# Linear attention into a GELU MLP on one core: a rebuilt opening with idle matmuls on zeros, own PSUM banks for the transposes, and two edits to the schedule of chunk preparation

## Chip, cores, metric

One core of a Trainium2 chip. The metric is the device time of one launch in microseconds (us), median of several runs. A profiled execution gives the trace. Its span, from the first to the last instruction, is some 2 us shorter than the time measured for the same execution.

## The reference

```python
# q, k, v: (4, 8, 768, 64); lam: (8,); w_in: (512, 2048); w_out: (2048, 512)
for b in range(nb):                       # blocks of 64 rows
    intra = (qb @ kb.T * Dmask) @ vb      # Dmask: lam**(i-j) on and below the diagonal
    inter = (qb * lam_pow) @ kv_state
    out[:, :, sl] = intra + inter
    kv_state = lam_block * kv_state + (kb * rev_pow).T @ vb
x = out, transposed to (3072, 512)
y = gelu_exact(x @ w_in) @ w_out          # (3072, 512), float32
```

## The kernel before

The kernel works in chunks of 128 rows: 24 chunks, six to a batch entry, so chunks 0, 6, 12 and 18 start from an empty state and chunks 5, 11, 17 and 23 need no new one. Four chunks make a group of 512 rows, which then goes through the MLP. The attention of the next group's chunks is woven between the MLP's matmuls of the present group.

Each chunk has these steps: loads of k, q, v on GpSimd's DMA queue; kT and qT (by TensorE for chunks 0 to 7, by a DMA transpose of k and of q_hat = q x decay for the later ones); k_dec = k x decay; scores; the product kv = k_decT v and the new state; outputs. GpSimd issues the loads and computes k_dec, q_hat and `old` (the decayed state). It executes all of this in program order.

The opening (chunks 0 to 3), cut:

```python
    def transposes(c):
        t_ps = bank([128, 2, HP, C], BF16, "mh" if c.early else "t", "t_ps")   # k and q in one bank
        ...
    def scores(c):        # scores, then kv, then masks, then the state: all in one function
        ...
    for s in range(M + 2):
        if s < M:
            live[s] = begin(s, early=True)
            if s == 2:
                load_w_in(0)
            transposes(live[s])
            decay_k(live[s], nc.scalar if s < 2 else nc.gpsimd)
            ...
        if 0 <= s - 1 < M:
            scores(live[s - 1])
        if s >= 2:
            outputs(live[s - 2], xT[0], s - 2)
```

The schedule of the later chunks, cut. A position is a fraction of a group's matmul work:

```python
    for n in range(M, NCH):
        g, i = n // M - 1, n % M
        first, end = (0.66, 1.0) if g == 0 else (0.0, 0.97)
        at = lambda f: (g + first + (end - first) * (i + f) / M) * total
        fs = (-0.5, 0.0, 0.5, 1.05) if g == 0 else (-1.0, 0.0, 0.35, 0.75)
        todo += [(at(f), kind, n) for kind, f in enumerate(fs)]
    todo.sort()

    def step(kind, n):
        g = n // M - 1
        if kind == 0:                      # preparation of chunk n
            live[n] = begin(n)
            if g > 0:
                dma_transposes(live[n])    # q_hat on GpSimd, two DMA transposes
            decay_k(live[n], nc.gpsimd)
            prefetch(n + 5)                # loads, up to that chunk
        ...
```

Of the kernel before, what the change touches and what calls it, by code (L numbers as in the profile page):

```python
# [8 lines left out]
F32 = mybir.dt.float32  # L9
BF16 = mybir.dt.bfloat16  # L10
ALU = mybir.AluOpType
ACT = mybir.ActivationFunctionType
# [3 lines left out]
def kernel(  # L16
# [10 lines left out]
    nc = tc.nc  # L27

    B, H, S, D = q.shape
    d_model, d_ff = moe_w_in.shape  # L30
    C = 128
    NB = S // C
    NCH = B * NB
    HP = H // 2
# [5 lines left out]
    M = 4  # L40
# [5 lines left out]
    consts = ctx.enter_context(tc.tile_pool(name="consts", bufs=1))  # L46
    w_pool = ctx.enter_context(tc.tile_pool(name="w", bufs=1))
    qkv_pool = ctx.enter_context(tc.tile_pool(name="qkv", bufs=8))
    work_pool = ctx.enter_context(tc.tile_pool(name="work", bufs=3))
# [13 lines left out]
    def load(n, name):  # L63
        raw[n, name] = qkv_pool.tile([128, H, D], BF16, tag=name, name=f"{name}_t")
        nc.gpsimd.dma_start(raw[n, name], chunk_of(name, n))  # L65
# [5 lines left out]
    pos = consts.tile([128, 1], F32)  # L71
# [13 lines left out]
    def load_w_in(s):  # L85
        f = d_ff // NS
        nc.gpsimd.dma_start(w_in_t[:, :, s * f:(s + 1) * f], w_in_r[:, :, s * f:(s + 1) * f])  # L87

    def load_w_out(s):
        f = NK2 // NS  # L90
        nc.gpsimd.dma_start(w_out_t[:, s * f:(s + 1) * f, :], w_out_r[:, s * f:(s + 1) * f, :])  # L91

    ident = consts.tile([128, 128], BF16)
    cmask = consts.tile([128, C], F32)
    negj = consts.tile([128, 1], F32)
    cmj = consts.tile([128, 1], F32)
    warm = consts.tile([128, 1], F32)
# [8 lines left out]
    lam_q = consts.tile([128, HP, C], F32)  # L106
# [3 lines left out]
    lam_c = consts.tile([128, HP], F32)  # L110
# [12 lines left out]
    lam_c_b = lam_c[:, :, None].to_broadcast((128, HP, D))  # L123

    def make_dmask():
        nc.vector.tensor_mul(dmask, cmask[:, None, :].to_broadcast((128, H, C)),
                             lam_m[:, :, None].to_broadcast((128, H, C)))
# [5 lines left out]
    xT = {}  # L133
    states = {}

    def bank(shape, dtype, tag, name):
        return ps.tile(shape, dtype, tag=tag, name=name, bufs=2 if tag in ("sc", "mh", "mo") else 1)

    def begin(n, early=False):
        c = Chunk()  # L140
        c.n, c.sb, c.early = n, n % NB, early
        c.sc_tag = "mo" if early and n % 2 else "sc"
        c.q, c.k, c.v = (raw.pop((n, name)) for name in "qkv")
        return c

    def decay_k(c, eng):

        if c.sb == NB - 1:
            return
        c.k_dec = work_pool.tile([128, H, D], BF16, tag="kd", name="k_dec")  # L150
        if eng is nc.scalar:
            for h in range(H):
                nc.scalar.activation(c.k_dec[:, h, :], c.k[:, h, :], ACT.Copy, scale=lam_k[:, h:h + 1])
        else:
            eng.tensor_mul(c.k_dec, c.k, lam_k[:, :, None].to_broadcast((128, H, D)))  # L155

    def transposes(c):
        t_ps = bank([128, 2, HP, C], BF16, "mh" if c.early else "t", "t_ps")
        for i, src in ((0, c.k), (1, c.q)):
            for hp in range(HP):  # L160
                nc.tensor.transpose(t_ps[:, i, hp, :], src[:, 2 * hp:2 * hp + 2, :], ident)  # L161
        c.kT = work_pool.tile([128, HP, C], BF16, tag="kT", name="kT")
        c.qT = work_pool.tile([128, HP, C], BF16, tag="qT", name="qT")
        if c.early:
            nc.scalar.copy(c.kT, t_ps[:, 0])
        else:
            nc.vector.tensor_copy(c.kT, t_ps[:, 0])  # L167
        nc.vector.tensor_mul(c.qT, t_ps[:, 1], lam_q)  # L168

    def dma_transposes(c):  # L170
        c.kT = work_pool.tile([128, HP, C], BF16, tag="kT", name="kT")
        c.qT = work_pool.tile([128, HP, C], BF16, tag="qT", name="qT")
        q_hat = work_pool.tile([128, H, D], BF16, tag="qh", name="q_hat")
        nc.sync.dma_start_transpose(out=c.kT, in_=c.k.rearrange("p h d -> p (h d)"))
        nc.gpsimd.tensor_mul(q_hat, c.q, lam_p[:, :, None].to_broadcast((128, H, D)))  # L175
        nc.sync.dma_start_transpose(out=c.qT, in_=q_hat.rearrange("p h d -> p (h d)"))

    def scores(c):
        sc_ps = [bank([128, HP, C], F32, c.sc_tag, f"sc_ps{hi}") for hi in range(2)]
        for hp in range(HP):  # L180
            for hi in range(2):
                p = slice(hi * D, (hi + 1) * D)
                nc.tensor.matmul(sc_ps[hi][:, hp, :], c.kT[p, hp, :], c.qT[p, hp, :], start=True, stop=True)  # L183
        more = c.sb < NB - 1
        if more:
            kv_ps = bank([128, HP, D], F32, "t", "kv_ps")
            for hp in range(HP):
                for hi in range(2):
                    h = 2 * hp + hi
                    nc.tensor.matmul(kv_ps[hi * D:(hi + 1) * D, hp, :], c.k_dec[:, h, :], c.v[:, h, :],  # L190
                                     start=True, stop=True)
        c.sc_m = work_pool.tile([128, HP, 2, C], BF16, tag="sc_m", name="sc_m")
        dmask_r = dmask.rearrange("p (hp hi) i -> p hp hi i", hi=2)
        for hi in range(2):
            nc.vector.tensor_mul(c.sc_m[:, :, hi, :], sc_ps[hi], dmask_r[:, :, hi, :])  # L195
        if more:
            new = work_pool.tile([128, HP, D], BF16, tag="state", name="state")
            if c.sb == 0:
                nc.vector.tensor_copy(new, kv_ps)
            else:  # L200
                nc.vector.tensor_add(new, kv_ps, states[c.n][1])  # L201
            old = work_pool.tile([128, HP, D], F32, tag="old", name="old")
            if c.sb < NB - 2:
                (nc.vector if c.early else nc.gpsimd).tensor_mul(old, new, lam_c_b)  # L204
            states[c.n + 1] = new, old

    def outputs(c, x_t, off):
        o_ps = bank([128, HP, C], F32, "o", "o_ps")
        if c.sb > 0:
            for hp in range(HP):  # L210
                for hi in range(2):
                    p = slice(hi * D, (hi + 1) * D)
                    nc.tensor.matmul(o_ps[p, hp, :], states[c.n][0][p, hp, :], c.qT[p, hp, :],  # L213
                                     start=(hp == 0), stop=False, skip_group_check=True)
        for hp in range(HP):
            for hi in range(2):
                nc.tensor.matmul(o_ps[hi * D:(hi + 1) * D, hp, :], c.v[:, 2 * hp + hi, :], c.sc_m[:, hp, hi, :],  # L217
                                 start=(c.sb == 0 and hp == 0), stop=True, skip_group_check=True)
        x_o = x_t[:, :, off * C:(off + 1) * C]
        if c.early:  # L220
            nc.scalar.copy(x_o, o_ps)  # L221
        else:
            nc.vector.tensor_copy(x_o, o_ps)  # L223
# [65 lines left out]
    def prefetch(upto):  # L289
        while next_load[0] <= min(upto, NCH - 1):  # L290
            for name in "kqv":
                load(next_load[0], name)
            next_load[0] += 1
# [2 lines left out]
    alloc_x(0)  # L296
    live = {}
    make_dmask()
    for s in range(M + 2):
        if s < M:  # L300
            live[s] = begin(s, early=True)
            if s == 2:
                load_w_in(0)
            transposes(live[s])
            decay_k(live[s], nc.scalar if s < 2 else nc.gpsimd)
            if s == 1:
                nc.scalar.activation(warm, pos, ACT.Gelu)
        if 0 <= s - 1 < M:
            scores(live[s - 1])
        if s >= 2:  # L310
            outputs(live[s - 2], xT[0], s - 2)
    for s in range(1, NS):
        load_w_in(s)
    for s in range(NS):
# [5 lines left out]
    for n in range(M, NCH):  # L320
        g, i = n // M - 1, n % M
        first, end = (0.66, 1.0) if g == 0 else (0.0, 0.97)
        at = lambda f: (g + first + (end - first) * (i + f) / M) * total
        fs = (-0.5, 0.0, 0.5, 1.05) if g == 0 else (-1.0, 0.0, 0.35, 0.75)
        todo += [(at(f), kind, n) for kind, f in enumerate(fs)]
    todo.sort()

    def step(kind, n):
        g = n // M - 1
        if kind == 0:  # L330
            live[n] = begin(n)
            if g > 0:
                dma_transposes(live[n])
            decay_k(live[n], nc.gpsimd)
            prefetch(n + 5)
        elif kind == 1:
            if g == 0:
                transposes(live[n])
        elif kind == 2:
            scores(live[n])  # L340
        else:
            outputs(live[n], xT[g + 1], n % M)

# [43 lines left out]
```

## Time and profile before

| | before |
|---|---|
| time, median of 3 runs | 239.39 us (237.59 to 240.59) |
| span of the profiled execution | 237.5 us |
| TensorE busy | 209.7 us |
| first large matmul (of the MLP) | 23.6 us |
| kv of chunk 4 | 46.8 us |
| kv of chunk 6, after a wait of 9.1 us for k_dec | 64.6 us |
| first large matmul of the second group | 73.6 us |
| scores of chunk 8 | 76.3 us |

Two of these from the timeline, kv of chunk 4 and the first large matmul of the second group:

```profile
46.84 0.32 PE L190 MATMUL kv_ps<-v_t,k_dec 128*64 128x64 bf16 x8
...
73.61 2.75 PE L235 MATMUL h_ps<-x_t,w_in_t 128*128 128x512 bf16 x12 [0.79 <-DVE x_t L223]
```

The strip in the prediction shows, in 40 slices of 5.94 us, the busy share in tenths and the clock granted to TensorE. The timeline has one row for each run of like instructions: start, duration, engine, line, operation, output<-inputs, shapes, count, and in brackets the idle time before it with what ended it. Line numbers shift between kernels; the tile names do not. "Cold" means that TensorE ran at half clock, "warm" at the full one.

### The profile page before, as it was taken

The numbers are of one execution on the slowest core, as the hardware profiler recorded it, in microseconds if no ns is written. First come the engines' busy times: TensorE is split into PE (matmuls) and PEld (weight loads), VectorE is DVE, ScalarE is ACT, GpSimd is POOL, SyncE is SP. The second block draws the span as 40 slices with busy tenths as digits, with TensorE's granted clock in tenths as the row PEclk, the third lists the DMA queues.
The fourth block names the chain that finished last, engine by engine and source line by source line (L and its number), as shares of the span: only waits on it lengthen the run. The fifth ranks groups of instructions, "written<-read, shape, count | busy, mean of one in ns | idle before, by whom it ended". The sixth has DMA issues, their size and how long they took to land.

```text
span 237.5 us, 3783 instructions
## 1 busy us (share of the span) xinstructions
PE 209.7 (88%) x1528; PEld 102.5 (43%) x1552; DVE 62.7 (26%) x111; ACT 86.0 (36%) x158; POOL 111.6 (47%) x132
## 2 busy tenths in 40 slices
PE   1576999993198999999999999999999999999994
PEld 0355344441044444444444444444444444444453
DVE  3396000264034333132223213222321323100000
ACT  6862365000004552106650125621056510266211
POOL 8997236899717949901684696004403200000000
PEclk9999999999569999999999999999999999999998
DMA  7999999999985999994969999601433101110012
GB/s 51 146 149 199 202 207 159 153 188 138 149 35 135 114 88 95 134 171 110 92 56 101 109 168 170 63 0 47 134 89 68 22 26 65 44 44 0 32 59 88
DMA packets 100272, 24.36 MB, mean 103 GB/s; under 512 B 92960, under 2 KB 97312, under 8 KB 100256
## 3 DMA queue, kind: packets, MB, share of 16 engines
q0 software_dynamic: 79104, 13.64, 79.7%
q1 hardware_dynamic: 21152, 10.50, 20.2%
q8 instruction: 12, 0.20, 0.4%
q14 instruction: 4, 0.03, 0.1%
HBM read 27.27 MB, written 6.29 MB: 141 GB/s over the span
## 4 chain that ended last, share of the span: by engine, by line
PE 70%; POOL 14%; DMA 11%; issue 3%; DVE 0%; ACT 0%; POOLq 0%
PE o_ps L247 30%; PE h_ps L235 30%; DMA w_out_t<-in_moe_w_out_dram 8%; DMA k_t<-in_k_dram 3%; POOL v_t L65 3%; POOL q_t L65 3%; POOL k_t L65 3%; PE o_ps L217 3%; PE sc_ps L183 2%; PE o_ps L213 2%; POOL k_dec L155 2%; PE kv_ps L190 2%; PE o_ps L262 1%; POOL w_in_t L87 1%; POOL w_out_t L91 1%
## 5 line engine op out<-in xcount | busy, mean ns | idle before, releaser
L235 PE MATMUL h_ps<-x_t,w_in_t 128*128 128x512 bf16 x372 | 88.0, 386 | 2.3 <-DVE x_t L223 0.8
L247 PE MATMUL o_ps<-w_out_t,g_t 128*128 128x512 bf16 x356 | 83.7, 385 | 1.8 <-issue 1.7
L237 ACT ACTIVATE g_t<-h_ps 128x512 bf16<-128x512 f32 x96 | 57.3, 597 | 41.0 <-PE h_ps L235 41.0
L235 PEld LDWEIGHTS <-w_in_t 128*128 128x128 bf16 x384 | 36.8, 99 | 45.5 <-issue 4.6
L247 PEld LDWEIGHTS <-g_t 128*128 128x128 bf16 x368 | 34.4, 99 | 40.4 <-issue 1.7
L252 ACT COPY o_sb<-o_ps 128x512 f32<-128x512 f32 x23 | 13.5, 585 | 96.0 <-PE o_ps L247 87.8
L195 DVE TENSOR_TENSOR sc_m<-sc_ps,dmask 128x512 bf16<-128x512 f32 x48 | 30.9, 685 | 62.5 <-PE sc_ps L183 62.5
L204 POOL TENSOR_TENSOR old<-state,lam_c 128x256 f32<-128x256 bf16 x12 | 7.3, 611 | 61.4 <-DVE state L201 35.3
L65 POOL DMA_DIRECT2D q_t<-in_q_dram x24 | 21.4, 894 | 5.4 <-DMA w_out_t<-in_moe_w_out_dram 3.3
L65 POOL DMA_DIRECT2D k_t<-in_k_dram x24 | 22.0, 915 | 3.7 <-DMA w_out_t<-in_moe_w_out_dram 1.7
L65 POOL DMA_DIRECT2D v_t<-in_v_dram x24 | 21.3, 889 | 5.0 <-DMA w_in_t<-in_moe_w_in_dram 1.7
L223 DVE CAST x_t<-o_ps 128x512 bf16<-128x512 f32 x20 | 13.8, 690 | 35.6 <-PE o_ps L217 35.6
L155 POOL TENSOR_TENSOR k_dec<-k_t,lam_k 128x512 bf16<-128x512 bf16 x18 | 19.0, 1058 | 0.0
L175 POOL TENSOR_TENSOR q_hat<-q_t,lam_p 128x512 bf16<-128x512 bf16 x16 | 16.7, 1046 | 0.0
L190 PE MATMUL kv_ps<-v_t,k_dec 128*64 128x64 bf16 x160 | 6.9, 212 | 10.5 <-POOL k_dec L155 9.1
L217 PE MATMUL o_ps<-sc_m,v_t 128*64 128x128 bf16 x192 | 10.8, 240 | 0.0
L183 PE MATMUL sc_ps<-qT,kT 64*128 64x128 bf16 x192 | 10.4, 233 | 0.3 <-DVE qT L168 0.2
L190 PEld LDWEIGHTS <-k_dec 128*64 128x64 bf16 x160 | 4.8, 119 | 12.9 <-POOL k_dec L155 9.3
L161 PE MATMUL t_ps<-ident,k_t 128*128 128x128 bf16 x32 | 4.2, 275 | 6.8 <-DMA k_t<-in_k_dram 6.3
L183 PEld LDWEIGHTS <-kT 64*128 64x128 bf16 x192 | 6.0, 99 | 9.5 <-issue 8.0
L213 PE MATMUL o_ps<-qT,state 64*64 64x128 bf16 x160 | 8.9, 235 | 0.7 <-ACT x_t L221 0.7
L167 DVE COPY kT<-t_ps 128x512 bf16<-128x512 bf16 x4 | 1.7, 424 | 28.2 <-PE t_ps L161 28.1
(39 smaller groups left out, 70.6 us busy)
## 6 DMA issues: line engine op xcount, KB each, us to landing
out_dram<-o_sb SPq DMA_DIRECT2D x23, 256.0 KB, 2.2
k_t<-in_k_dram POOLq DMA_DIRECT2D x24, 128.0 KB, 4.4
q_t<-in_q_dram POOLq DMA_DIRECT2D x24, 128.0 KB, 5.5
v_t<-in_v_dram POOLq DMA_DIRECT2D x24, 128.0 KB, 6.1
w_in_t<-in_moe_w_in_dram POOLq DMA_DIRECT2D x4, 512.0 KB, 8.4
w_out_t<-in_moe_w_out_dram POOLq DMA_DIRECT2D x4, 512.0 KB, 15.4
kT<-k_t SPq DMA_TRANSPOSE x16, 4.0
qT<-q_hat SPq DMA_TRANSPOSE x16, 4.1
```

Of the source, the lines that this page charges most:

```text
L65: nc.gpsimd.dma_start(raw[n, name], chunk_of(name, n))
L155: eng.tensor_mul(c.k_dec, c.k, lam_k[:, :, None].to_broadcast((128, H, D)))
L175: nc.gpsimd.tensor_mul(q_hat, c.q, lam_p[:, :, None].to_broadcast((128, H, D)))
L183: nc.tensor.matmul(sc_ps[hi][:, hp, :], c.kT[p, hp, :], c.qT[p, hp, :], start=True, stop=True)
L190: nc.tensor.matmul(kv_ps[hi * D:(hi + 1) * D, hp, :], c.k_dec[:, h, :], c.v[:, h, :], start=True, stop=True)
L195: nc.vector.tensor_mul(c.sc_m[:, :, hi, :], sc_ps[hi], dmask_r[:, :, hi, :])
L213: nc.tensor.matmul(o_ps[p, hp, :], states[c.n][0][p, hp, :], c.qT[p, hp, :], start=(hp == 0), stop=False, skip_group_check=True)
L217: nc.tensor.matmul(o_ps[hi * D:(hi + 1) * D, hp, :], c.v[:, 2 * hp + hi, :], c.sc_m[:, hp, hi, :], start=(c.sb == 0 and hp == 0), stop=Tru ...
L223: nc.vector.tensor_copy(x_o, o_ps)
L235: nc.tensor.matmul(h_ps, w_in_t[:, ki, kf * 128:(kf + 1) * 128], x_t[:, ki, :], start=(ki == 0), stop=(ki == NK1 - 1))
L237: nc.scalar.activation(g_t[:, kf, :], h_ps, ACT.Gelu)
L247: nc.tensor.matmul(om[io], g_t[:, kf, io * C:(io + 1) * C], w_out_t[:, kf, :], start=(kf == 0), stop=(kf == NK2 - 1))
```

## The change

The intent by its title: TensorE should not wait idle, and at a halved clock, while the first chunks arrive. The diff has two edits more, in the schedule. Its core:

```diff
+    idle = consts.tile([128, 512], BF16)
+    nc.vector.memset(idle, 0.0)
...
     def transposes(c):
-        t_ps = bank([128, 2, HP, C], BF16, "mh" if c.early else "t", "t_ps")
+        if c.early:
+            t_ps = [bank([128, HP, C], BF16, tag, "t_ps") for tag in ("mh", "mo")]
...
-        if c.early:
-            nc.scalar.copy(c.kT, t_ps[:, 0])
-        else:
-            nc.vector.tensor_copy(c.kT, t_ps[:, 0])
+        if c.early and c.n > 0:
+            nc.scalar.copy(c.kT, t_ps[0])
+        else:
+            nc.vector.tensor_copy(c.kT, t_ps[0])
...
+    def next_state(c):          # kv and the new state, taken out of scores(); early: old on ScalarE
...
+    def keep_warm(n):
+        for _ in range(n):
+            nc.tensor.matmul(idle_ps, idle[:, :128], idle, start=True, stop=True)
+    keep_warm(9)
+    early(0)
+    keep_warm(4)
+    scores(live[0])
+    keep_warm(4)
+    early(1)
+    keep_warm(2)
+    next_state(live[0])
+    outputs(live[0], xT[0], 0)
+    scores(live[1])
+    load_w_in(0)
+    early(2)
+    next_state(live[1])
+    early(3)
+    outputs(live[1], xT[0], 1)
+    scores(live[2])
...
-        fs = (-0.5, 0.0, 0.5, 1.05) if g == 0 else (-1.0, 0.0, 0.35, 0.75)
+        fs = (-0.5, 0.0, 0.5, 1.05) if g == 0 else (-0.45 if n == 2 * M else -1.0, 0.0, 0.35, 0.75)
...
-            prefetch(n + 5)
+            prefetch(n + 4)
```

More of the change, by code (lines that the diff above doesn't have):

```diff
@@ L141, in begin @@
         c.n, c.sb, c.early = n, n % NB, early
-        c.sc_tag = "mo" if early and n % 2 else "sc"
         c.q, c.k, c.v = (raw.pop((n, name)) for name in "qkv")
@@ L157, in transposes @@
     def transposes(c):
-        t_ps = bank([128, 2, HP, C], BF16, "mh" if c.early else "t", "t_ps")
-        for i, src in ((0, c.k), (1, c.q)):
+        if c.early:
+            t_ps = [bank([128, HP, C], BF16, tag, "t_ps") for tag in ("mh", "mo")]
+        else:
+            both = bank([128, 2, HP, C], BF16, "t", "t_ps")
+            t_ps = [both[:, 0], both[:, 1]]
+        for dst, src in zip(t_ps, (c.k, c.q)):
             for hp in range(HP):
-                nc.tensor.transpose(t_ps[:, i, hp, :], src[:, 2 * hp:2 * hp + 2, :], ident)
+                nc.tensor.transpose(dst[:, hp, :], src[:, 2 * hp:2 * hp + 2, :], ident)
         c.kT = work_pool.tile([128, HP, C], BF16, tag="kT", name="kT")
         c.qT = work_pool.tile([128, HP, C], BF16, tag="qT", name="qT")
-        if c.early:
-            nc.scalar.copy(c.kT, t_ps[:, 0])
-        else:
-            nc.vector.tensor_copy(c.kT, t_ps[:, 0])
-        nc.vector.tensor_mul(c.qT, t_ps[:, 1], lam_q)
+        if c.early and c.n > 0:
+            nc.scalar.copy(c.kT, t_ps[0])
+        else:
+            nc.vector.tensor_copy(c.kT, t_ps[0])
+        nc.vector.tensor_mul(c.qT, t_ps[1], lam_q)
     def dma_transposes(c):
@@ L178, in scores @@
     def scores(c):
-        sc_ps = [bank([128, HP, C], F32, c.sc_tag, f"sc_ps{hi}") for hi in range(2)]
+        sc_ps = [bank([128, HP, C], F32, "sc", f"sc_ps{hi}") for hi in range(2)]
         for hp in range(HP):
@@ L183, in scores @@
                 nc.tensor.matmul(sc_ps[hi][:, hp, :], c.kT[p, hp, :], c.qT[p, hp, :], start=True, stop=True)
-        more = c.sb < NB - 1
-        if more:
-            kv_ps = bank([128, HP, D], F32, "t", "kv_ps")
-            for hp in range(HP):
-                for hi in range(2):
-                    h = 2 * hp + hi
-                    nc.tensor.matmul(kv_ps[hi * D:(hi + 1) * D, hp, :], c.k_dec[:, h, :], c.v[:, h, :],
-                                     start=True, stop=True)
         c.sc_m = work_pool.tile([128, HP, 2, C], BF16, tag="sc_m", name="sc_m")
@@ L195, in scores @@
             nc.vector.tensor_mul(c.sc_m[:, :, hi, :], sc_ps[hi], dmask_r[:, :, hi, :])
-        if more:
-            new = work_pool.tile([128, HP, D], BF16, tag="state", name="state")
-            if c.sb == 0:
-                nc.vector.tensor_copy(new, kv_ps)
-            else:
-                nc.vector.tensor_add(new, kv_ps, states[c.n][1])
-            old = work_pool.tile([128, HP, D], F32, tag="old", name="old")
-            if c.sb < NB - 2:
-                (nc.vector if c.early else nc.gpsimd).tensor_mul(old, new, lam_c_b)
-            states[c.n + 1] = new, old
+    def next_state(c):
+        if c.sb == NB - 1:
+            return
+        kv_ps = bank([128, HP, D], F32, "t", "kv_ps")
+        for hp in range(HP):
+            for hi in range(2):
+                h = 2 * hp + hi
+                nc.tensor.matmul(kv_ps[hi * D:(hi + 1) * D, hp, :], c.k_dec[:, h, :], c.v[:, h, :],
+                                 start=True, stop=True)
+        new = work_pool.tile([128, HP, D], BF16, tag="state", name="state")
+        if c.sb == 0:
+            nc.vector.tensor_copy(new, kv_ps)
+        else:
+            nc.vector.tensor_add(new, kv_ps, states[c.n][1])
+        old = work_pool.tile([128, HP, D], F32, tag="old", name="old")
+        if c.early:
+            for hp in range(HP):
+                nc.scalar.activation(old[:, hp, :], new[:, hp, :], ACT.Copy, scale=lam_c[:, hp:hp + 1])
+        elif c.sb < NB - 2:
+            nc.gpsimd.tensor_mul(old, new, lam_c_b)
+        states[c.n + 1] = new, old
     def outputs(c, x_t, off):
@@ L298, with early @@
     make_dmask()
-    for s in range(M + 2):
-        if s < M:
-            live[s] = begin(s, early=True)
-            if s == 2:
-                load_w_in(0)
-            transposes(live[s])
-            decay_k(live[s], nc.scalar if s < 2 else nc.gpsimd)
-            if s == 1:
-                nc.scalar.activation(warm, pos, ACT.Gelu)
-        if 0 <= s - 1 < M:
-            scores(live[s - 1])
-        if s >= 2:
-            outputs(live[s - 2], xT[0], s - 2)
+    nc.scalar.activation(warm, pos, ACT.Gelu)
+    def early(s):
+        live[s] = begin(s, early=True)
+        transposes(live[s])
+        decay_k(live[s], nc.scalar if s < 2 else nc.gpsimd)
+    idle_ps = bank([128, 512], F32, "o", "idle_ps")
+    def keep_warm(n):
[17 more added lines that the diff above has]
+    scores(live[2])
+    next_state(live[2])
+    outputs(live[2], xT[0], 2)
+    scores(live[3])
+    outputs(live[3], xT[0], 3)
+    next_state(live[3])
     for s in range(1, NS):
@@ L340, in step @@
             scores(live[n])
+            next_state(live[n])
         else:
```

## The prediction

> **What bounds the kernel now.** I read the page's strip of 40 slices first, then the waits of TensorE, then the timeline at each place where TensorE was idle, then what GpSimd and the DMA queue did there. One slice of the strip is 5.94 us.
>
> ```profile
> PE   1576999993198999999999999999999999999994
> POOL 8997236899717949901684696004403200000000
> PEclk9999999999569999999999999999999999999998
> ```
>
> TensorE is the bound nearly everywhere: 209.7 of 237.5 us busy, and 158.6 of the 163.9 us after 73.6 us. It is idle in two places only: the opening (slices 1 to 4) and a hole at 53 to 65 us (slices 10 and 11). Behind the hole the clock is low for two slices. The waits of TensorE name the hole:
>
> ```profile
> PE kv_ps L190 <- POOL k_dec L155: 9.1, 1, 9.1
> PE t_ps L161 <- DMA k_t<-in_k_dram: 6.3, 3, 4.9
> PE t_ps L161 <- DMA q_t<-in_q_dram: 2.0, 4, 1.3
> ```
>
> It is one wait of 9.1 us, for a decayed k. The timeline shows which one and why:
>
> ```profile
> 52.00 1.08 POOL L175 TENSOR_TENSOR q_hat<-q_t,lam_p 128x512 bf16<-128x512 bf16 x1
> 53.00 1.07 POOL L155 TENSOR_TENSOR k_dec<-k_t,lam_k 128x512 bf16<-128x512 bf16 x1
> ...
> 60.75 0.87 POOL L65 DMA_DIRECT2D q_t<-in_q_dram  x1 [0.57 <-DMA v_t<-in_v_dram]
> 62.58 0.87 POOL L65 DMA_DIRECT2D v_t<-in_v_dram  x1 [0.95 <-DMA k_t<-in_k_dram]
> 63.46 2.05 POOL L155 TENSOR_TENSOR k_dec<-k_t,lam_k 128x512 bf16<-128x512 bf16 x2
> 64.57 0.43 PE L190 MATMUL kv_ps<-v_t,k_dec 128*64 128x64 bf16 x8 [9.11 <-POOL k_dec L155]
> ```
>
> The k_dec at 63.46 is that of chunks 6 and 7; chunk 6 had landed at about 47 us (its loads' issue times plus times to landing in the DMA view). It is late because GpSimd works in program order. The schedule puts chunk 8's preparation (position 0.7575 of a group) ahead of chunk 6's (0.7875), and that step prefetches up to chunk 13: nine loads at some 0.88 us of GpSimd each, the last two also held back by a full DMA queue. The hole costs more than its length:
>
> ```profile
> 55.50:64.60 9.10, 0.03 (x2) 0.03 (x2) 1.29 (x2) 0.00 (x0) 7.55 (x10) 0.68 2.88 147
> 64.60:69.00 4.40, 4.40 (x23) 2.13 (x24) 0.42 (x1) 0.00 (x0) 1.52 (x2) 0.50 1.72 72
> ```
>
> (Stretch, length, busy time of PE, PEld, DVE, ACT, POOL, granted clock, DMA share, GB/s.) After the hole TensorE is fully busy, but at clock 0.50.
>
> The opening also ends cold:
>
> ```profile
> 23.60 0.59 PE L235 MATMUL h_ps<-x_t,w_in_t 128*128 128x512 bf16 x1 [0.68 <-ACT x_t L221]
> 24.41 15.37 PE L235 MATMUL h_ps<-x_t,w_in_t 128*128 128x512 bf16 x61 [0.22 <-issue]
> 25.26 0.15 PEld L235 LDWEIGHTS <-w_in_t 128*128 128x128 bf16 x1 [0.28 <-issue]
> 25.69 0.15 PEld L235 LDWEIGHTS <-w_in_t 128*128 128x128 bf16 x1 [0.28 <-issue]
> 28.17 11.11 PEld L235 LDWEIGHTS <-w_in_t 128*128 128x128 bf16 x52 [0.20 <-issue]
> ```
>
> Weight loads come every 0.43 us up to 28.2, then every 0.21. The strip's 9 before that is no warm clock: four transposes take 0.61 us there and 0.39 later. I trust the spacing.
>
> **What the Trainium skill says.** "TensorE: Matmul & The Clock Gate", Part 1 (the clock gate): the array's clock is halved until about 3.4 us of sustained activity, and after about one idle window of that length. The trace agrees: 0.427 against 0.216 us per 512-column matmul, and the clock record falls to 0.5 at 58.8, 3.3 us into the hole, until 69.0. Part 4 of that page says that transposes don't count as busy in the same way. That fits an opening which never warms, though no record here separates transposes. "PSUM — Partial Sum Buffer", Terms: two engines must not touch one bank at once. The trace agrees: qT (VectorE, 8.03) starts when kT (ScalarE, 7.42 plus 0.58) is done, and kT itself waited for q's transposes, although k's had ended at 5.49. "DMA: Bandwidth & Descriptors", Issuing engines are not separate DMA queues: transfers from all engines share the same 16 DMA engines. The trace agrees: chunk 8's qT transpose, issued by SyncE at 53.1 among chunk loads, took 7.3 us to land against a median of 4.1.
>
> **The change, part by part.** The diff does more than its short title.
>
> (a) **Prefetch n+4 for n+5, and chunk 8's preparation at -0.45 for -1.0** (position 0.891 for 0.7575, behind chunk 7's at 0.8725). This is the large part. GpSimd's order becomes: k_dec4, loads 8, loads 9, k_dec6, loads 10, k_dec7, loads 11, old6, q_hat8, k_dec8, loads 12. The first twelve loads of this stage (chunks 4 to 7) stay behind the weights and are held by the full queue as now, so k_dec4 still starts at 42.9. From there, with 1.05 us per k_dec or q_hat, 2.65 per three loads and 0.61 per old: k_dec4 ends 44.0, loads 9 end 49.4, **k_dec6 ends 50.4**, loads 10 end 53.0, k_dec7 54.1, loads 11 56.7, old6 57.3, **q_hat8 58.4**. TensorE reaches kv of chunk 6 at 55.4 today, so the 9.1 us wait goes away. With it goes the cold stretch: 8 matmuls x (0.427 - 0.216) = 1.7 us, and about 0.35 on the transposes and outputs up to 69.0. Together 11.2 us.
>
> (b) **The opening.** 19 idle matmuls of 512 columns: 19 x 0.427 = 8.1 us cold, 4.1 warm. The first nine (3.8 us, from about 1.2 to 5.0) lie in the 4.88 us that TensorE waits for the first k anyway. The other ten stand in order in front of real work: 4.3 us cold, 2.2 warm. Separate banks let kT0 (now on VectorE) start at about 6.4 instead of 7.42 and qT0 at about 7.5 instead of 8.03; scores of chunk 0 no longer wait behind chunk 1's transposes (10.01 today). ScalarE gets old: 4 chunks x 4 small activations, each some 0.25 us by k_dec's (eight in 2.02 us), 4 us in all beside copies on the same engine. I walked the four chunks through all engines with these durations. If the clock stays cold, the first large matmul comes at about 23.9 (23.6 today); if it is warm by 8 us, at about 21.1, and then without the 1.9 us of cold large matmuls (9 x 0.21). w_in's first quarter lands at 19.7 (issue 11.97 plus 7.7), so it doesn't bind.
>
> (c) **What of (b) counts.** kv of chunk 4 is at 46.84 today. A warm opening brings TensorE there at about 41.3, but k_dec4 is done at 44.0. So the opening can give at most 46.84 - 44.1 = 2.7 us; cold, it gives about 0 to 1. The rest becomes a new wait.
>
> (d) **The next wait.** From kv4 to kv6 TensorE needs 8.6 us (46.84 to 55.4), from kv6 to the scores of chunk 8 11.7 (64.57 to 76.30), less the 2.1 that was cold: 9.6. So scores 8 come 18.2 after kv4: at 62.3 to 64.5. Their qT needs q_hat8 (58.4) and the DMA transpose: 4.1 us at the median gives 62.5, 7.3 under load gives 65.7. I choose scores 8 at 64.3, against 76.30 today: **12.0 us less**. What follows, 161 us of nearly full TensorE, stays as it is; loads still come some three chunk slots ahead of use.
>
> 239.4 - 12.0 = 227.4; I put **227.0 us**.
>
> **Rivals.**
> - The opening alone matters and the middle stays (the title's reading): 2.7 us at most, 236.5 us. Against it: the 9.1 us wait is made by the order on GpSimd that the diff changes.
> - Idle matmuls get in the way, clock cold: ten in front of real work cost 4.3 us. For it: the queue is in order, and today's opening never warmed. Against it: most fall in waits for q and k. It would leave kv4 near 46.8, scores 8 near 65, 228 us.
> - GpSimd and the DMA queue become the bound in the middle: qT8 lands after 65.7, or k_dec6 is pushed behind a full queue. For it: nine loads and two transposes share the engines, and times to landing are 6 to 9 us there. 229 to 232 us; a hole over 3.4 us would also cool the clock again.
> - Everything fits and qT8 comes early: 62.3, a gain of 14, 225.4 us; with more saved at the start, 223.
>
> **Range and chances.** The three runs of before spread by 3 us, and the free end of the DMA transposes gives 3 more, so 222.5 to 231.5. The hole is certain to shrink by its cause; to lose the 4.8 us that make 2%, a new hole of over 7 us would have to appear. Faster 0.94, same 0.05, slower 0.01.
>
> **What would show it.** No wait of over 4 us of kv on k_dec of chunk 6; k_dec6 by about 51 us; no record of clock 0.5 between 50 and 75. A wait of some 0 to 3 us of kv4 on k_dec4 near 44 if the opening got warm, with the first large matmul near 21 and spaced 0.216; near 24 and 0.427 if not. A wait of 0 to 3 us at scores 8 for a DMA transpose. Span about 225. I am wrong if chunk 4's k_dec moves by several us either way (then the DMA order is not what holds GpSimd), if scores 8 wait much longer, or if the steady groups after 80 us show new holes from the shorter prefetch.

## The result

The changed kernel takes 226.36 us (median of 4, 225.31 to 226.47) against 239.99 us (median of 4, 237.59 to 241.51) for the kernel before. The ratio is 0.9454, interval 0.9372 to 0.9536.

The strip of the changed kernel (a slice is 5.61 us):

```profile
PE   7767999989899999999999999999999999999993
POOL 8998333899999895045955992042141100000000
PEclk9995699999999999999999999999999999999999
```

The hole in the middle of TensorE's row is gone, and so is the low clock behind it. Slices 4 and 5, in the opening, show another low clock. (The opening of the kernel before was cold up to 28.1 us, by its spacing; its record begins only there.) The waits of TensorE (waiting engine, tile, line, releaser: us in total, times, longest) no longer name k_dec at all:

```profile
PE t_ps L167 <- DMA q_t<-in_q_dram: 2.0, 4, 1.0
...
PE t_ps L167 <- DMA k_t<-in_k_dram: 1.4, 2, 1.2
PE idle_ps L321 <- DVE idle L94: 1.2, 1, 1.2
```

The timeline of the changed kernel in the middle shows the new order on GpSimd and what TensorE makes of it:

```profile
44.99 0.32 PE L202 MATMUL kv_ps<-v_t,k_dec 128*64 128x64 bf16 x8
...
49.67 1.09 POOL L156 TENSOR_TENSOR k_dec<-k_t,lam_k 128x512 bf16<-128x512 bf16 x1
...
53.35 1.07 POOL L156 TENSOR_TENSOR k_dec<-k_t,lam_k 128x512 bf16<-128x512 bf16 x1
...
53.54 0.32 PE L202 MATMUL kv_ps<-v_t,k_dec 128*64 128x64 bf16 x8
...
57.60 1.05 POOL L181 TENSOR_TENSOR q_hat<-q_t,lam_p 128x512 bf16<-128x512 bf16 x1
...
58.68 1.20 SPq L182 DMA_TRANSPOSE qT<-q_hat  x1
...
60.46 2.75 PE L245 MATMUL h_ps<-x_t,w_in_t 128*128 128x512 bf16 x12 [0.79 <-DVE x_t L233]
...
63.14 0.40 PE L189 MATMUL sc_ps<-qT,kT 64*128 64x128 bf16 x8
```

These rows are kv of chunk 4, k_dec of chunk 6 (done 2.8 us before TensorE needs it), k_dec of chunk 7, kv of chunk 6 without a wait, q_hat of chunk 8, its transpose (4.3 us to landing, so 63.0), the first large matmul of the second group, and the scores of chunk 8 at 63.14. That transpose and the scores come out almost together.

The milestones side by side, from the two traces:

| milestone | before | changed | earlier by |
|---|---|---|---|
| first large matmul | 23.60 | 21.75 | 1.85 |
| kv of chunk 4 | 46.84 | 44.99 | 1.85 |
| kv of chunk 6 | 64.57 | 53.54 | 11.03 |
| first large matmul, second group | 73.61 | 60.46 | 13.15 |
| end of the span | 237.5 | 224.4 | 13.1 |

So 1.85 us come from the opening, 9.2 from the wait of kv of chunk 6 (11.03 less 1.85), and 2.1 from the cold stretch that followed it (13.15 less 11.03). From the second group's first large matmul to the end both kernels need 163.9 us.

The clock in the opening is a story of its own. Windows of the changed kernel (start:end, length, busy time and count on PE, PEld, DVE, ACT, POOL, granted clock, DMA share, GB/s):

```profile
5.75:9.17 3.42, 2.50 (x21) 1.26 (x22) 2.48 (x5) 3.40 (x12) 3.42 (x5) 1.00 2.23 142
9.17:12.58 3.41, 2.46 (x41) 1.43 (x40) 2.74 (x5) 3.41 (x15) 3.41 (x5) 1.00 2.35 150
12.58:15.99 3.41, 1.97 (x37) 1.30 (x38) 1.75 (x4) 3.32 (x11) 2.88 (x4) 1.00 1.83 148
15.99:19.40 3.41, 2.89 (x44) 1.96 (x41) 2.00 (x5) 1.70 (x6) 3.41 (x6) 0.50 1.18 185
```

The idle matmuls did free the clock, at 5.8 us. TensorE was then busy for 72 to 73% of a window, and the clock stayed; in the window from 12.58 it was busy for 58%, and at 16.0 the clock was halved again, until 26.2. The busy share alone does not decide this: the kernel with the position edit alone (experiment 4) kept a free clock through two windows of 54% and 56% (59.98 to 63.39 to 66.80), filled mostly by large matmuls. As the clock was halved from 16.0 on, the first large matmuls still run at the slow spacing, 0.43 us between weight loads up to 26.0:

```profile
21.75 0.59 PE L245 MATMUL h_ps<-x_t,w_in_t 128*128 128x512 bf16 x1 [0.46 <-ACT x_t L231]
...
25.54 0.15 PEld L245 LDWEIGHTS <-w_in_t 128*128 128x128 bf16 x1 [0.28 <-issue]
...
25.97 0.15 PEld L245 LDWEIGHTS <-w_in_t 128*128 128x128 bf16 x1 [0.28 <-issue]
26.32 3.77 PEld L245 LDWEIGHTS <-w_in_t 128*128 128x128 bf16 x18 [0.20 <-issue]
```

### The profile page after: what moved, and what is told of

It reads as the page before. It is cut to its first block, busy times and chain, and to the rows that moved or that the text cites. A ratio compares the mean times of both kernels' runs of the same rounds, so it can differ in the third digit from the quotient of the medians.

```text
span 224.4 us, 3835 instructions
## 1 busy us (share of the span) xinstructions
PE 210.8 (94%) x1547; PEld 101.7 (45%) x1571; DVE 61.2 (27%) x109; ACT 89.1 (40%) x173; POOL 111.4 (50%) x132
## 4 chain that ended last, share of the span: by engine, by line
PE 76%; DMA 12%; POOL 8%; issue 2%; DVE 0%; ACT 0%; POOLq 0%
PE o_ps L257 33%; PE h_ps L245 31%; DMA w_out_t<-in_moe_w_out_dram 8%; PE o_ps L227 3%; PE sc_ps L189 3%; PE o_ps L223 3%; DMA k_t<-in_k_dram 2%; POOL q_t L65 2%; DMA v_t<-in_v_dram 2%; PE kv_ps L202 2%; POOL k_t L65 2%; PE o_ps L272 2%; POOL v_t L65 2%; POOL w_in_t L87 1%; POOL w_out_t L91 1%
## 5 line engine op out<-in xcount | busy, mean ns | idle before, releaser
L257 PE MATMUL o_ps<-w_out_t,g_t 128*128 128x512 bf16 x356 | 82.0, 379 | 1.8 <-issue 1.7
L223 PEld LDWEIGHTS <-state 64*64 64x64 bf16 x160 | 5.4, 110 | 7.6 <-issue 7.3
L173 DVE COPY kT<-t_ps 128x512 bf16<-128x512 bf16 x5 | 2.1, 423 | 23.5 <-PE t_ps L167 23.4
L227 PEld LDWEIGHTS <-v_t 128*64 128x64 bf16 x192 | 6.4, 112 | 3.3 <-issue 1.6
L321 PE MATMUL idle_ps<-idle 128*128 128x512 bf16 x19 | 6.7, 498 | 1.2 <-DVE idle L94 1.2
```

Source lines behind the costliest of these rows:

```text
L223: nc.tensor.matmul(o_ps[p, hp, :], states[c.n][0][p, hp, :], c.qT[p, hp, :], start=(hp == 0), stop=False, skip_group_check=True)
L227: nc.tensor.matmul(o_ps[hi * D:(hi + 1) * D, hp, :], c.v[:, 2 * hp + hi, :], c.sc_m[:, hp, hi, :], start=(c.sb == 0 and hp == 0), stop=Tru ...
L257: nc.tensor.matmul(om[io], g_t[:, kf, io * C:(io + 1) * C], w_out_t[:, kf, :], start=(kf == 0), stop=(kf == NK2 - 1))
```

## Experiments

All kernels gave the right result. My theory: nearly all the gain comes from GpSimd's order in the middle, and what the opening can add is capped there, first by k_dec of chunk 4 and then by qT of chunk 8. The rival, after the title: the opening makes the gain, or the parts simply add. Each group of four kernels was timed on one chip with shared runs of the kernel before. A trace is of one of the timed executions, and not always of a typical one: it was the slowest of its run for the kernels of experiments 3, 4 and 7 and for the first of experiment 6, and the fastest for the last kernel of experiment 6, both times.

### 1. The changed kernel again

> The changed kernel once more, as the reference point for the others on this chip: 226.4 us, ratio to before about 0.945, kv of chunk 4 at 45.0, scores of chunk 8 at 63.1. The rival (a lucky draw of the clock's phase in the first runs) would put it off by over 1 us.

Measured: 225.99 us against 239.93, ratio 0.9421 (0.9388 to 0.9454). In its trace, kv of chunk 4 is at 44.68 and the scores of chunk 8 at 62.83. On a second chip (`after_ref`) it took 226.08 us, ratio 0.9414:

> The changed kernel as reference on the chip of these runs: 226.0 us, first large matmul at about 21.6, kv of chunk 4 at about 44.8.

The result repeats. In that profiled execution the clock fell only for the window from 20.0 to 23.4, the first large matmul came at 20.80, and TensorE could have had kv of chunk 4 at 43.2. The profile shows what it did instead (timeline):

```profile
44.76 0.32 PE L202 MATMUL kv_ps<-v_t,k_dec 128*64 128x64 bf16 x8 [1.57 <-POOL k_dec L156]
```

It waited 1.57 us for k_dec of chunk 4, and its span, 224.0 us, is hardly shorter. This is the cap of the prediction's part (c), caught in one execution of the unaltered kernel. The scores of chunk 8 (62.75) waited 0.41 us for qT there, so the wait of part (d) occurs too.

### 2. The two schedule edits alone

```diff
# kernel before
-        ... else (-1.0, 0.0, 0.35, 0.75)
+        ... else (-0.45 if n == 2 * M else -1.0, 0.0, 0.35, 0.75)
-            prefetch(n + 5)
+            prefetch(n + 4)
```

> The kernel before with the two schedule edits alone (prefetch n+4, chunk 8's preparation at -0.45). My theory: the hole goes, kv of chunk 4 stays at 46.8, kv of chunk 6 comes at 55.4 without a wait, scores of chunk 8 at about 65.0, 228.2 us, so 11.3 of the 13.1 us. Rival (the rebuilt opening is the main part, as its title has it): under half of the gain, 233 us or more.

Measured: 228.27 us, ratio 0.9501 (0.9468 to 0.9533). Its timeline has kv of chunk 4, kv of chunk 6 and the scores of chunk 8 so:

```profile
46.44 0.32 PE L190 MATMUL kv_ps<-v_t,k_dec 128*64 128x64 bf16 x8
...
54.98 0.32 PE L190 MATMUL kv_ps<-v_t,k_dec 128*64 128x64 bf16 x8
...
64.59 0.40 PE L183 MATMUL sc_ps<-qT,kT 64*128 64x128 bf16 x8
```

No wait stands before any of them. Two edited lines give 11.7 of the 13.9 us between the medians of before and changed on this chip.

### 3. The new opening alone

The changed kernel with those two lines as before.

> The changed kernel with the two schedule edits taken back: the new opening alone. My theory: the opening's 1.9 us are lost in the hole, as its end is set by GpSimd's order: k_dec of chunk 6 still ends at about 64.5 to 65, the wait of kv on it grows from 9.1 to about 11, and the time stays within 1 us of before (239 to 240). Rival (the parts add up): 1.9 us less than before, 237.5 to 238.

Measured: 239.08 us against 239.93, ratio 0.9952 (0.9917 to 0.9987). The timeline at kv of chunk 6:

```profile
64.54 0.42 PE L202 MATMUL kv_ps<-v_t,k_dec 128*64 128x64 bf16 x8 [10.86 <-POOL k_dec L156]
```

TensorE arrives earlier and waits longer, 10.9 us in place of 9.1, and gets kv at 64.54 against 64.57 before. The 1.8 us of the opening are lost in the hole. Some 0.9 us of difference remain between the medians; in the profiled execution they are not found, so what makes them stays open. There, the low clock behind the hole even lasted four windows (56.75 to 70.41) against three before (58.81 to 69.05), and the second group's first large matmul came at 74.16, later than the 73.61 of before. The parts don't add: the same opening is worth 0.9 us in front of the hole and 2.3 us (228.27 less 225.99) without it.

### 4. Which of the two schedule edits

The changed kernel with the prefetch back at n+5, and the changed kernel with the position back at -1.0.

> The changed kernel with the prefetch taken back to n+5; chunk 8's preparation stays at -0.45. GpSimd then does loads 8, 9, 10 before k_dec of chunk 6: k_dec6 ends at 53.5, q_hat8 at 61.5, its transpose lands at about 65.8. Theory: the large hole stays away (wait at kv of chunk 6 under 1 us), but scores of chunk 8 wait some 2.7 us for qT: 228 to 229 us. Rival (the distance of the prefetch makes the hole): near 236 us.

> The changed kernel with chunk 8's preparation taken back to -1.0; prefetch stays n+4. GpSimd again puts q_hat8, k_dec8 and nine loads ahead of k_dec of chunk 6, which ends at 61 to 62.5. Theory (the position is the cause): kv of chunk 6 waits 7 to 9 us and the clock is lost: 234.5 to 237.5 us. Rival (the distance of the prefetch makes the hole): 226 to 228 us.

Measured: with the position edit alone 228.38 us, ratio 0.9530; with the prefetch edit alone 236.45 us, ratio 0.9861 (0.9818 to 0.9905). The latter shows, in its timeline, that the hole is back:

```profile
62.36 0.43 PE L202 MATMUL kv_ps<-v_t,k_dec 128*64 128x64 bf16 x8 [8.82 <-POOL k_dec L156]
```

So the position of chunk 8's preparation closes the hole: 10.5 us (236.45 less 225.99). The prefetch edit is worth 2.4 us beside it (228.38 less 225.99). The 225.99 is from another chip (experiment 1); by the ratios to before, 0.9421 there, the two are 10.5 and 2.6 us. I had expected these as one wait for qT of chunk 8. The waits of TensorE in the kernel with the position edit alone show two:

```profile
PE h_ps L245 <- DVE x_t L233: 1.8, 1, 1.8
PE o_ps L257 <- issue: 1.7, 11, 0.2
PE sc_ps L189 <- DMA qT<-q_hat: 1.5, 1, 1.5
```

The second is the expected one (q_hat at 60.4 to 61.4, transpose 4.2 us). The first is longer than the 0.8 us of the changed kernel by 1.0: `old` of chunk 6, on GpSimd behind three more loads, ends at 60.4, and VectorE, which works in program order, waits 1.28 us for it before the state and then the copy x_t that the large matmuls need.

### 5. No idle matmuls

The changed kernel without its 19 idle matmuls, their tile and the memset.

> The changed kernel without the 19 idle matmuls. Theory one (the clock they win at 5.8 us is lost again at 16.0, before the large matmuls, and the opening follows the arrival of the chunks): first large matmul at 21.5 to 22.3, cold until about 26, time within 0.7 us of the changed kernel. Theory two (the warm stretch is what brings the 1.9 us): first large matmul at 23 to 23.6, kv of chunk 4 near 46.5, 1.3 to 1.9 us slower than the changed kernel.

Measured: 226.70 us, ratio 0.9440 (0.9410 to 0.9469), against 225.99 and 0.9421 for the changed kernel in the same rounds. The intervals overlap. In the trace the first large matmul comes at 22.70 (20.80 to 22.52 in the three traces of the changed kernel) and kv of chunk 4 at 45.42, 0.4 to 0.7 us later than in those traces. The time is at the edge of theory one's range, and 22.70 lies between the ranges of the two, nearer the first: the idle matmuls that the title names are worth some 0.7 us here, if that. The rest of the rebuilt opening is worth more, some 1.6 us (228.27 of experiment 2 less 226.70). Which of its edits makes that (own banks, copies and `old` on other engines, the new order, the earlier load of ScalarE's GELU table) no run separates. The trace of the changed kernel shows only that qT of chunk 0 starts at 7.18, where it had waited until 8.03 before.

### 6. A clock that stays up, and the caps behind it

18 further idle matmuls, put where TensorE waited between 12.8 and 21.7 us, into banks that are free there:

```diff
     next_state(live[1])
+    keep_warm(5, bank([128, 512], F32, "sc", "idle_sc"))
     early(3)
+    more_idle = bank([128, 512], F32, "mo", "idle_mo")
     outputs(live[1], xT[0], 1)
     scores(live[2])
     next_state(live[2])
+    keep_warm(5, more_idle)
     outputs(live[2], xT[0], 2)
     scores(live[3])
+    keep_warm(6, more_idle)
     outputs(live[3], xT[0], 3)
     next_state(live[3])
+    keep_warm(2, more_idle)
```

> 18 more idle matmuls where TensorE waits between 12.8 and 21.7 us, so that the clock is not lost at 16.0. The clock should stay at 1.0 and the large matmuls start warm at about 21.4. Theory (step c of the prediction: k_dec of chunk 4, done at 44.4, is the cap): TensorE could be at kv of chunk 4 at 42.4 but waits there some 2 us for k_dec; kv at 44.5, gain 0.3 to 0.6 us. Rival (no cap): kv of chunk 4 at 42.4, 2.5 us less, 223.5 us. If the idle matmuls get in the way: slower than the changed kernel.

Measured: 226.30 us, ratio 0.9406, against 226.08 and 0.9414: the same. Yet in the profiled execution the clock stayed at 1.0 once it was free, at 10.1 us, and the large matmuls started warm at 21.75. The timeline says where it went:

```profile
45.85 0.32 PE L202 MATMUL kv_ps<-v_t,k_dec 128*64 128x64 bf16 x8 [2.65 <-POOL k_dec L156]
```

TensorE is there 2.65 us before k_dec of chunk 4, which GpSimd computes behind the loads of chunks 4 to 7. In this execution it started at 44.74; in the other traces with this order at 42.3 to 44.0. The trace shows GpSimd held in front of it by loads that wait 1.7 us each for earlier transfers of w_in and w_out; what sets the spread stays open.

The next kernel issues k_dec of chunk 4 ahead of chunk 7's loads:

```diff
-    prefetch(2 * M - 1)
+    prefetch(2 * M - 2)
+    live[M] = begin(M)
+    decay_k(live[M], nc.gpsimd)
+    prefetch(2 * M - 1)
...
         if kind == 0:
-            live[n] = begin(n)
-            ...
+            if n > M:
+                ...
```

> As e6_all_warm, with k_dec of chunk 4 issued on GpSimd ahead of chunk 7's loads. kv of chunk 4 then at about 42.4 with hardly a wait. Theory (step d: the next cap is qT of chunk 8, q_hat at 58.6 plus 4.3 us of transpose, 63.0): scores of chunk 8 would want to start at 60.6 and wait about 2.4 us, total gain over the changed kernel still under 0.7 us. Rival (no second cap): scores of chunk 8 at 60.6, 223.5 us.

Measured: 225.36 us, ratio 0.9387 (0.9348 to 0.9427), so less than the changed kernel by 0.7 us, with overlapping intervals. The first cap is gone and the second stands where it was expected (timeline: kv of chunk 4, scores of chunk 8):

```profile
42.69 0.32 PE L202 MATMUL kv_ps<-v_t,k_dec 128*64 128x64 bf16 x8
...
62.26 0.40 PE L189 MATMUL sc_ps<-qT,kT 64*128 64x128 bf16 x8 [1.33 <-DMA qT<-q_hat]
```

kv of chunk 4 is 2.3 us earlier than in the first trace of the changed kernel, and 1.33 of them are waited away at the scores of chunk 8. The wait was to be 2.4; q_hat came somewhat earlier and its transpose took 4.0 us.

The last kernel of this line also puts q_hat of chunk 8 ahead of k_dec of chunk 7:

```diff
+        if n == 2 * M:
+            todo.append((at(-0.62), 4, n))      # q_hat and the transposes alone
...
+        elif kind == 4:
+            live[n] = begin(n)
+            dma_transposes(live[n])
```

> As e7_kdec4_early, with q_hat of chunk 8 on GpSimd ahead of k_dec of chunk 7 (at about 54.4), so that its transpose lands by 60. With both caps lifted the warm opening's 2.5 us should come through: scores of chunk 8 at 60.6 to 61.5, 223.5 to 224.3 us. If neither cap was real: the same as e6 and e7.

> The kernel with both caps lifted and the warm opening once more, as reference for e9: ratio to before 0.937 to 0.939, about 225.0 us.

Measured: 224.98 us, ratio 0.9386, and on another chip 225.13 us, ratio 0.9403. So its median is about 1 us below that of the changed kernel (226.0 to 226.1), and the intervals of the ratios overlap. It is above the 223.5 to 224.3 us expected, and its ratio is that of the kernel without this edit (0.9387), so that lifting the second wait gains time is not shown. The first trace:

```profile
42.63 0.32 PE L202 MATMUL kv_ps<-v_t,k_dec 128*64 128x64 bf16 x8
...
61.37 0.40 PE L189 MATMUL sc_ps<-qT,kT 64*128 64x128 bf16 x8
```

No wait stands at the scores now, but they are at 61.37, not 60.6: the first large matmul of the second group waits 1.38 us for x_t, where the changed kernel waited 0.79. It is the wait of experiment 4 again: VectorE waits 0.88 us for `old` of chunk 6. The kernel falls in two kinds of execution as well. In 8 of the 12 the mean clock was 0.997 or more and the span 222.2 to 223.5 us; in 4 it was 0.990 to 0.992 and the span 224.6 to 225.0. A mean clock of 0.992 over 224 us is 3.6 us at half clock. (The mean counts the time before the first change of the record as full clock: it was 0.997 or more in the kernel of experiment 7 too, cold until 27.3 us in its trace. So it does not show when a clock was first freed.) I have no trace of one of those four, so where the window lay is open.

### 7. The caps lifted, without idle matmuls

> As e8_both_early (k_dec of chunk 4 and q_hat of chunk 8 early) but with no idle matmul at all. Theory: once the caps are gone, a cold clock at the first large matmuls costs its full length: first large matmul at 22.7, cold until about 26, kv of chunk 4 at 45.0 to 45.5, 226.3 us, 1.2 to 2 us slower than e8; the idle matmuls, worth 0.7 us or less in the changed kernel, would be worth that here. Rival (the clock in the opening is of no matter): within 0.5 us of e8.

Measured: 226.08 us, ratio 0.9428 (0.9390 to 0.9465), against 225.13 and 0.9403 (0.9360 to 0.9446) for the kernel with them in the same rounds: 1.0 us, between the two expectations, with overlapping intervals. Its first large matmul is at 22.45, its clock record starts at 27.3, and kv of chunk 4 is at 45.89, so in the traces the warm opening is worth 3.4 us there (42.48 in the other). But these traces are of the slowest and of the fastest execution (227.34 and 224.18), so that is no typical figure. The mean span of its six executions is 224.3 us; that of the eight above is 222.8. So a clock kept up would be worth some 1.4 us once the caps are lifted. That is likely rather than shown, as those eight are chosen by their mean clock, and traces show the clock kept up in two of them only.

## Why the prediction was right

**The hole (part a).** k_dec of chunk 6 was to end at 50.4 and ended at 50.8; q_hat of chunk 8 at 58.4, and 58.6. The gain of 11.2 us from hole and cold stretch was 11.3 (13.15 less 1.85), and experiment 2 has it alone, 11.7 by the medians. The position edit does it (experiment 4), as the prediction had it: it named the order of chunks 8 and 6 first.

**The opening (part b)** came out between its two cases. I had the clock either cold throughout (first large matmul at 23.9) or free from 8 us on (21.1, and large matmuls warm). It was free at 5.8 and lost at 16.0: first matmul at 21.75, large matmuls cold until 26.2. I had left out that a thin opening can lose the clock again. No run shows the cold case as it was put, with the idle matmuls in the way; without them, cold throughout, the first large matmul came at 22.5 to 22.7. The steps for chunk 0 held: kT at 6.30 and qT at 7.18, against 6.4 and 7.5.

**The cap (part c)** is real. k_dec of chunk 4 was to start at 42.9; it started at 43.39, and TensorE arrived at 44.99, just after it was done. Where TensorE came earlier, by the clock's luck or by more idle matmuls, it waited 1.57 and 2.65 us there (experiments 1 and 6). With a warm clock up to the large matmuls it came there at 42.5 to 43.2 (experiment 6), not at 41.3.

**The next wait (part d)** was over-sized. I chose 64.3 us for the scores of chunk 8; they were at 63.14 and did not wait, as the transpose took 4.3 us, near the median of before, not 7.3. So the gain at that milestone was 13.16 us, not 12.0. The prediction's own sum, 227.4, less these 1.16 us gives 226.2, against 226.36 measured; the step from 227.4 to the 227.0 that was put has no working. The wait is real where something comes later or earlier: 0.41 us in experiment 1, 1.5 in experiment 4, 1.33 in experiment 6.

**The rivals.** "The opening alone" was put at 236.5 us and measured 239.08: I had charged the hole in its place but not seen that a fixed end of the hole swallows an earlier start. Idle matmuls in front of real work did not lengthen anything that a run shows; they fell into waits, as held against that rival. No new hole came from the shorter prefetch: the rest of the kernel takes 163.9 us in both.

## What to carry to other kernels

Where an engine both issues transfers and computes, read its program order at the start of every hole: the wait names the late product, and the cause is what stood in front of it. An early gain is worth what is left of it at the next wait that something else ends, so follow milestones through the trace, and count on parts not adding: the same opening gave 0.9 us before the hole was closed and 2.3 after. If a clock is to be freed by idle work, the idle work has to reach as far as the work that is to profit, and the caps behind it have to go too.

## What the Trainium skill lacked or had wrong

- "TensorE: Matmul & The Clock Gate", Part 1, says that a busy window frees the clock and an idle one halves it, but not how busy. In the changed kernel's opening, windows with TensorE busy for 72 to 73% kept a free clock (2.50 and 2.46 of 3.4 us), and one with 58% (1.97 us), without a gap of over 1.3 us, lost it. The kind of matmul counts as well. Two windows of 54% and 56%, mostly large matmuls, kept the clock in experiment 4. Windows of small matmuls and transposes did not free it at 2.90 of 3.40 us busy in the kernel before, nor at 94% (15.90 to 19.31) in the one without idle matmuls. The stretches in the records are whole multiples of 3.413 us (16.0 to 26.2, 10.24, is three; 28.1 to 58.8 in the kernel before, 30.72, is nine), as the page's window length has it.
- The same page doesn't say whether matmuls on zeros count as activity. They do: in the first trace of experiment 1 the clock was freed at 4.3 us, when TensorE had run nothing but the first nine idle matmuls, from 1.19 us on. With the same nine it was freed at 5.8 us in the first trace, and only at 9.9 and 10.1 us in two others.
- Part 4 of that page says that transposes don't engage the fast clock. Four of them took 0.61 us at the slow clock and 0.39 at the fast one here, so they do run faster on it. Whether they help to free it is not separated by a run.
- The page warns that clock records can be unreliable, but no page has this: the record starts with the first change, so the strip showed 9 for the first 28 us of the kernel before, which ran at half speed by its spacing (0.427 us per 512 columns against 0.216).
- "DMA: Bandwidth & Descriptors", Issuing engines are not separate DMA queues, calls the sequencer's time to start a DMA usually small relative to the DMA itself. On GpSimd it was about 0.88 us for each 128 KB load, against 5.0 to 6.2 us from issue to landing (medians of the changed kernel). What the section leaves out is the work behind it on the same engine: nine loads in a row (8 us of issuing) stood in front of one 1.05 us product, and TensorE's wait for it, 9.1 us, was the longest of the kernel before.
